# Reordering the first DMA issues of a fused attention and soft mixture-of-experts kernel

## The chip, the cores and the metric

The kernel runs on one core of a Trainium2 chip. The metric is the device time of one execution in microseconds (us); the times given are medians over a few executions. TensorE (PE) multiplies matrices, with its weight loads shown apart as PEld; VectorE (DVE), ScalarE (ACT) and GpSimd (POOL) do the element work; SyncE (SP) only issues DMAs here, and ScalarE's queue can issue DMAs as well. In the profile, SP's DMA queue is q1 and ScalarE's is q10.

## The reference

```python
# q, k, v: (4, 5056, 256) float32; tau: a scalar (1.0)
qn = q / (np.linalg.norm(q, axis=1, keepdims=True) + 1e-06)
kn = k / (np.linalg.norm(k, axis=1, keepdims=True) + 1e-06)
s = kn.transpose(0, 2, 1) @ qn / tau            # (4, 256, 256)
a = softmax(s, axis=-1)
x = (v @ a).reshape(4 * 5056, 256)
# phi: (256, 32); w1: (8, 256, 1024); w2: (8, 1024, 256)
logits = x @ phi
d = softmax(logits, axis=0)
slot_input = (d.T @ x).reshape(8, 4, 256)
slot_out[e] = np.maximum(slot_input[e] @ w1[e], 0) @ w2[e]   # e = 0..7
out = softmax(logits, axis=1) @ slot_out.reshape(32, 256)
```

The softmaxes subtract the maximum and add 1e-9 to the sum. Everything is in float32.

## The kernel before

The rows of q and k are cut into 40 **units** (ten for each of four batches). A unit is one tile `raw` of 128 partitions, four row groups `j` of q and k side by side: 8 KB a partition, 1 MB in all. Five buffers of `raw` exist (`NRAW = 5`), so units 0 to 4 are loaded at once and each later load waits until its buffer's readers are done. For each unit:

- ScalarE squares the whole tile into `sq` (line 203) for the column norms, and VectorE adds the squares up (line 209).
- Of units 1 to 39, row groups 0 and 1 are split into a rounded part (ScalarE, `cast`, line 182) and a rest (VectorE, `low`, line 188), both in the tile `hl`; three products on `hl` replace one on `raw`.
- TensorE adds the products of k and q into the score bank `S` (line 226), directly from `raw` for the row groups that are not split. Unit 0 has none split (`NS[0] = 0`): its eight products, in order of `j`, all read `raw`. A float32 product stands in the trace as two records of a weight load and two of a matmul.

In between run the loads of v and of its transpose (lines 128 and 134), the softmax over the scores, the logits, the gather of the slots, and at the end the two layers of the experts (`w1`, line 626; `w2`, line 631), the output products (line 712), their copies to SBUF on ScalarE and VectorE (lines 734 and 736) and the stores (lines 742 and 744).

The work of the main part is entered in a list `plan` by `at(key, function, arguments)`, and issued in the order of the written-out list `ORDER` of indices into `plan`. What stands outside the plan is issued ahead of it: the loads of units 0 to 4 first, then a few constants and `act.activation(warm, ...)`, which loads ScalarE's function table (line 154). Each engine, and each DMA queue, takes its own instructions in the order in which they are issued.

Three places matter here. Unit 0 is loaded in two parts, row group 0 by ScalarE's queue and groups 1 to 3 by SP's (line 141). A burst of `WAKE = 6` products of a tile of ones (`wake`, line 749) is entered first in the plan; nothing reads its result. The small tile `few_sb` holds phi, a selection mask and tau for each partition, 268 bytes a partition; it is loaded on SP by `load_few` (line 139), entry 646 of the plan, which stands 52nd in `ORDER`. Its first reader is VectorE's reciprocal of tau (line 258), and then TensorE's product with phi (line 319).

Of the kernel before, what the change touches and what calls it, by code (L numbers as in the profile page):

```python
# [8 lines left out]
F32 = mybir.dt.float32  # L9
# [7 lines left out]
P, S, G = 128, 32, 4  # L17
UB = 10
PB = 5
UT = 512  # L20
WAKE = 6
PITCH = 128
NU = B * UB
NRAW = 5
# [4 lines left out]


ORDER = [
# [46 lines left out]
]  # L78


# [1 line left out]
def colnorm_attention_soft_moe(  # L82
# [15 lines left out]
    pe, act, dve, pool, sp = nc.tensor, nc.scalar, nc.vector, nc.gpsimd, nc.sync  # L98
    ctx.enter_context(tc.manual_schedule())

    const = ctx.enter_context(tc.tile_pool(name="const", bufs=1))
# [13 lines left out]
    def load_qk(u, parts=((0, 4, sp),)):  # L115
        b, i = divmod(u, UB)
        raw = apool.tile([P, 4, 2, C], F32, tag="raw", name=f"raw{u}", bufs=NRAW)
        for lo, hi, queue in parts:
            src = qk[b, i][:, : 8 * C].rearrange("p (j x c) -> p j x c", x=2, c=C)
            queue.dma_start(raw[:, lo:hi], src[:, lo:hi])  # L120
        raws[u] = raw
# [13 lines left out]
        else:  # L135
            sp.dma_start(t[:, : 8 * P - HD], vt7[b, m])

    def load_few():
        sp.dma_start(few_sb, few)

    load_qk(0, ((0, 1, act), (1, 4, sp)))
    for u in range(1, NRAW):
        load_qk(u)

# [7 lines left out]
    dve.memset(half, 0.5)  # L152
    warm = const.tile([P, 1], F32, name="warm")
    act.activation(warm, ones[:, 0:1], AF.Exp)
    few_sb = const.tile([P, 2 * S + 3], F32, name="few_sb")
    phi_sb = few_sb[:, : 2 * S].rearrange("p (n s) -> p n s", n=2)
    sel_sb = few_sb[:, 2 * S : 2 * S + 2]
    rtau = const.tile([P, 1], F32, name="rtau")
# [595 lines left out]
    def at(key, f, *a):  # L754
        plan.append((key, len(plan), f, a))

    at(-2, wake, WAKE)
    FV = 13
# [96 lines left out]
    for p in range(17):  # L855
        k = (4, 6, 8, 10, 12, 15)[p] if p < 6 else 2 * p + 7
        for h in range(2):
# [3 lines left out]
            if h:  # L861
                for m in range(2):
                    if (p, m) in LT:
                        at(k + h + 0.996 + 0.001 * m, load_vt, p, m)
    at(3.5, load_few)

    T0_ = [NU + 1.0]

# [191 lines left out]
```

## Time and profile before

| | |
|---|---|
| median of 3 runs | 288.36 us (287.0 to 289.2) |
| the profiled execution | 287.02 us |
| its span, first to last instruction | 285.2 us |
| TensorE / VectorE / ScalarE busy | 249.9 / 236.5 / 185.0 us |
| moved by DMA | 115.61 MB, 405 GB/s on average |
| mean granted TensorE clock | 0.961 |

A profile page belongs to one execution. Times inside it count from the first instruction, and the 1.8 us between the span and the execution's time lie around it. In the page's slices, each digit is the busy share of one fortieth of the span in tenths. In a timeline row the first number is the start, the second the duration from the first to the last of the merged instructions, then engine, line, operation, tiles and count; the bracket tells how long the engine was idle before and what ended that. ACTq and SPq are the sequencers of ScalarE and SyncE, where DMAs are issued. In rows of groups, after the bar, stand the busy time and the mean duration of one in ns.

### The profile page before, as it was taken

To read this page: it belongs to the slowest core of one execution; us is meant where nothing else is said; L and a number is where in the kernel's file an instruction comes from. 1 tells how busy PE (TensorE), PEld (TensorE's weight loads), DVE (VectorE), ACT (ScalarE), POOL (GpSimd) and SP (SyncE) were. 2 spreads that over 40 slices of the span, in tenths; PEclk is the share of its full clock that TensorE was granted. 3 is DMA by queue.
4 is the path that set the end of the run, shared out by engine and by line. 5 is a ranking of instruction groups with operands and counts; after the bars stand their busy time and mean duration, and the time that the engine had idled before them with its cause. 6 is when DMAs were issued, how large, how long until landed. Compare 5 with 4: busy or idle time off the path is not lost. (4 is left out here: it accounts for less than half of the span.)

```text
span 285.2 us, 6082 instructions
## 1 busy us (share of the span) xinstructions
PE 249.9 (88%) x2446; PEld 202.5 (71%) x2446; DVE 236.5 (83%) x389; ACT 185.0 (65%) x264; POOL 9.8 (3%) x10
## 2 busy tenths in 40 slices
PE   5999999999999999999999999999889898984000
PEld 5899999897898978878778686786454777753000
DVE  1699999899999999999999999978768688994100
ACT  3978897889899796687777967175613436862200
POOL 0000002200003000000200000100000000000000
PEclk9999999999999999999999999999999999999555
DMA  7999999999999999999999999999999998999995
GB/s 277 426 411 421 413 425 420 420 417 418 400 418 388 419 434 419 416 408 410 418 398 418 411 418 430 421 425 418 422 412 415 413 371 325 407 423 416 424 424 244
DMA packets 20044, 115.61 MB, mean 405 GB/s; under 512 B 2352, under 2 KB 2352, under 8 KB 9520
## 3 DMA queue, kind: packets, MB, share of 16 engines
q1 hardware_dynamic: 19872, 114.96, 98.1%
q8 instruction: 19, 0.31, 0.4%
q10 hardware_dynamic: 144, 0.26, 0.3%
q14 instruction: 9, 0.07, 0.1%
HBM read 94.24 MB, written 20.97 MB: 404 GB/s over the span
## 5 line engine op out<-in xcount | busy, mean ns | idle before, releaser
L209 DVE TENSOR_TENSOR sq<-sq,sq 128x1024 f32<-128x1024 f32 (+1 forms) x63 | 85.3, 1367 | 1.3 <-ACT sq L203 0.6
L203 ACT ACTIVATE sq<-raw 128x2048 f32<-128x2048 f32 x40 | 76.3, 1911 | 14.5 <-DVE sq L209 5.8
L226 PE MATMUL S<-raw 128*128 128x256 f32 x328 | 81.6, 391 | 1.9 <-DMA raw<-in_qk_dram 1.9
L226 PE MATMUL S<-hl 128*128 128x256 f32 x468 | 71.0, 297 | 0.1
L226 PEld LDWEIGHTS S<-raw 128*128 128x128 f32 x328 | 60.5, 195 | 12.3 <-issue 3.3
L226 PEld LDWEIGHTS S<-hl 128*128 128x128 f32 x468 | 61.1, 190 | 3.2 <-issue 1.2
L188 DVE TENSOR_TENSOR hl<-raw,hl 128x1024 fp32r<-128x1024 f32 x39 | 47.0, 1215 | 7.1 <-ACT hl L182 7.1
L182 ACT CAST hl<-raw 128x1024 fp32r<-128x1024 f32 x39 | 40.2, 1042 | 3.3 <-PE S L226 2.6
L736 DVE COPY o<-op_None 128x512 f32<-128x512 f32 x30 | 18.7, 676 | 7.9 <-issue 7.2
L734 ACT COPY o<-op_None 128x512 f32<-128x512 f32 x30 | 15.8, 593 | 12.5 <-issue 8.2
L712 PE MATMUL op_None<-so,cT 32*128 32x256 f32 x240 | 18.6, 401 | 1.9 <-ACT o L734 1.3
L485 PE MATMUL G<-v,dn 128*32 128x256 f32 x320 | 20.1, 382 | 0.1
L712 PEld LDWEIGHTS op_None<-so,cT 32*128 32x128 f32 x240 | 14.6, 184 | 5.6 <-ACT o L734 2.7
L378 PE MATMUL L<-vt,M 128*32 128x256 f32 (+1 forms) x272 | 17.7, 380 | 0.9 <-ACT M L332 0.9
L356 ACT COPY vt<-vTp 128x512 f32<-128x512 f32 x18 | 10.4, 584 | 11.3 <-PE vTp L351 11.3
L248 POOL TENSOR_TENSOR rn<-rn,half 128x4 f32<-128x4 f32 x4 | 9.1, 2264 | 173.7 <-DVE rn L243 173.7
L485 PEld LDWEIGHTS G<-v,dn 128*32 128x32 f32 x320 | 10.0, 109 | 6.6 <-issue 0.5
L351 PE MATMUL vTp<-ident,v 128*128 128x128 f32 x96 | 14.2, 277 | 0.1
L378 PEld LDWEIGHTS L<-vt,M 128*32 128x32 f32 x272 | 8.1, 109 | 6.9 <-ACT M L332 1.3
L351 PEld LDWEIGHTS vTp<-ident,v 128*128 128x128 f32 x96 | 11.0, 142 | 2.6 <-issue 1.2
L399 ACT COPY lt<-L 128x256 f32<-128x256 f32 x20 | 7.2, 372 | 7.6 <-DVE mxs L405 3.4
L734 ACT COPY o<-op 128x256 f32<-128x256 f32 x20 | 6.3, 380 | 7.1 <-PE op L712 7.1
(111 smaller groups left out, 249.3 us busy)
## 6 DMA issues: line engine op xcount, KB each, us to landing
raw<-in_qk_dram SPq DMA_DIRECT2D x39, 1024.0 KB, 8.4
v<-in_v_dram SPq DMA_DIRECT2D x20, 1024.0 KB, 9.8
out_dram<-o SPq DMA_DIRECT2D x15, 1024.0 KB, 12.3
vt<-in_vt_dram SPq DMA_DIRECT2D x21, 512.0 KB, 8.4
w<-in_moe_w_dram SPq DMA_DIRECT2D x8, 1024.0 KB, 13.9
w<-in_moe_w_dram SPq DMA_DIRECT2D x16, 512.0 KB, 10.0
out_dram<-o SPq DMA_DIRECT2D x10, 512.0 KB, 4.2
vt<-in_vt_dram SPq DMA_DIRECT2D x4, 480.0 KB, 8.8
```

The source lines that it names most:

```text
L182: act.copy(hl[:, :ns, 0::2, :], raws[u][:, :ns])
L188: dve.tensor_tensor(hl[:, :ns, 1::2, :], raws[u][:, :ns], hl[:, :ns, 0::2, :].bitcast(F32), op=ALU.subtract)
L203: act.activation(sq, raws[u], AF.Square)
L209: dve.tensor_tensor(a[:, lo:hi], a[:, lo:hi], s[:, lo:hi], op=ALU.add)
L226: pe.matmul(sm, w, x, start=first, stop=False, skip_group_check=True)
L351: pe.transpose(tp[:, P * jj : P * jj + P], vs[p][:, 4 * h + jj, P * m : P * m + P], ident)
L356: act.copy(x[:, h * UT : h * UT + UT], tps[p, h, m])
L378: pe.matmul(L[S * g : S * g + S, :n, :], M[:, m, :], x[:, :n, S * g : S * g + S], start=m == 0, stop=m == 1,)
L485: pe.matmul(gp[S * g : S * g + S, :C], dn[:, x, j, :], vt[:, j, :], start=x == 0 and j < G, stop=x == n - 1 and j >= G,)
L712: pe.matmul(ops[b, p, hf, g][:, h, :], cT[b][S * g : S * g + S, 4 * i : 4 * i + 4, :].rearrange("s j t -> s (j t)"), so[S * g : S * g + S] ...
L734: act.copy(dst, src)
L736: dve.tensor_copy(dst, src)
```

## The change

The load of `few_sb` moves out of the plan to the very front, onto ScalarE's queue, as its first DMA. Unit 0 is cut in the middle: SP's queue opens with row groups 0 and 1, and ScalarE issues groups 2 and 3 behind `few_sb`. The plan's entry for `load_few` is gone, so the indices above 646 in `ORDER` fall by one; the order of all the other entries is the same as before. `WAKE` goes from 6 to 5.

```diff
-WAKE = 6
+WAKE = 5
...
 ORDER = [
-    ... 49, 44, 646, 52, 58, ...
+    ... 49, 44, 52, 58, ...
...
-    def load_few():
-        sp.dma_start(few_sb, few)
-
-    load_qk(0, ((0, 1, act), (1, 4, sp)))
+    few_sb = const.tile([P, 2 * S + 3], F32, name="few_sb")
+    act.dma_start(few_sb, few)
+    load_qk(0, ((0, 2, sp), (2, 4, act)))
     for u in range(1, NRAW):
         load_qk(u)
...
     act.activation(warm, ones[:, 0:1], AF.Exp)
-    few_sb = const.tile([P, 2 * S + 3], F32, name="few_sb")
     phi_sb = few_sb[:, : 2 * S].rearrange("p (n s) -> p n s", n=2)
...
-    at(3.5, load_few)
```

90 rows, old and new, of the table ORDER are left out of this document.

## The prediction

> **What bounds the kernel now.** I read the page first: the span and its busy lines, then its slices.
>
> ```profile
> span 285.2 us, 6082 instructions
> PE 249.9 (88%) x2446; PEld 202.5 (71%) x2446; DVE 236.5 (83%) x389; ACT 185.0 (65%) x264; POOL 9.8 (3%) x10
> PE   5999999999999999999999999999889898984000
> DVE  1699999899999999999999999978768688994100
> DMA  7999999999999999999999999999999998999995
> ```
>
> Three resources are full side by side: TensorE and VectorE from the second slice to about the thirtieth, the DMA engines from the second to the last. A table of stretches separates the stages (columns: PE, PEld, DVE, ACT, POOL busy, TensorE clock, DMA share, GB/s).
>
> ```profile
> 1.70:2.80 1.10, 1.10 (x7) 1.10 (x7) 0.59 (x6) 0.95 (x2) 0.00 (x0) 1.00 0.84 143
> 2.80:5.80 3.00, 1.18 (x6) 0.88 (x5) 0.00 (x0) 0.00 (x0) 0.00 (x0) 1.00 1.04 428
> 16.00:72.00 56.00, 55.88 (x382) 50.60 (x381) 54.27 (x51) 47.47 (x45) 3.07 (x1) 1.00 1.01 419
> 92.00:228.00 136.00, 132.10 (x1358) 100.29 (x1357) 124.77 (x236) 86.48 (x143) 2.99 (x2) 1.00 1.02 417
> 228.00:248.00 20.00, 18.20 (x375) 15.07 (x370) 17.25 (x40) 12.18 (x32) 0.00 (x0) 1.00 0.92 363
> 248.00:280.00 32.00, 10.67 (x138) 8.18 (x130) 13.10 (x24) 9.67 (x19) 0.00 (x0) 0.73 1.01 422
> ```
>
> From 16 to 72 us TensorE idles 0.12 us of 56 and VectorE 1.73 us, with DMA at 419 GB/s. From 248 us on the stores drain at 422 GB/s and nothing but the queue matters. Only between 228 and 248 us does DMA fall, to 363 GB/s, because stores wait for output tiles. So the end is the moment at which the output tiles are made, plus a fixed drain, and that moment is the end of a chain that runs through TensorE from its first product. A gain at the head reaches the end only if TensorE, VectorE and the load stream all let it through.
>
> The change touches the head alone. Its timeline:
>
> ```profile
> 0.73 0.40 ACTq L120 DMA_DIRECT2D raw<-in_qk_dram  x1
> 0.74 13.95 SPq L120 DMA_DIRECT2D raw<-in_qk_dram  x7
> 1.05 2.93 PE L749 MATMUL wake<-ones 128*128 128x128 f32 x12 [1.05 <-DVE half L152]
> 1.17 1.28 ACT L154 ACT_TABLE_LOAD   x1 [1.17 <-PEq L1017]
> 2.46 0.20 ACT L154 ACTIVATE warm<-ones 128x1 f32<-128x1 f32 x1
> 5.85 1.91 ACT L203 ACTIVATE sq<-raw 128x2048 f32<-128x2048 f32 x1 [3.19 <-DMA raw<-in_qk_dram]
> 5.87 10.14 PE L226 MATMUL S<-raw 128*128 128x256 f32 x36 [1.89 <-DMA raw<-in_qk_dram]
> 8.14 1.04 ACT L182 CAST hl<-raw 128x1024 fp32r<-128x1024 f32 x1 [0.38 <-DMA raw<-in_qk_dram]
> 11.03 2.29 DVE L209 TENSOR_TENSOR sq<-sq,sq 128x2048 f32<-128x2048 f32 x1 [0.59 <-ACT sq L203]
> ```
>
> TensorE runs the products of ones until 3.98 us, idles 1.89 us and starts when unit 0 is there; ScalarE starts with it, then idles 0.38 us for unit 1. VectorE follows ScalarE. From here TensorE has no idle time in the timeline.
>
> **The change, part by part.**
>
> *The split of unit 0.* Both of its DMAs leave within 0.01 us of each other and land 4.9 and 5.1 us later, at about 5.64 and 5.83 us:
>
> ```profile
> L120 SPq DMA_DIRECT2D raw<-in_qk_dram x5: 371/424/779, 0.7 to 2.9; - x5
> DMA to landing us min/median/max: 4.9/5.0/5.1
> q1 hardware_dynamic: 116, 0.71, 69.5%
> q10 hardware_dynamic: 108, 0.22, 21.1%
> ```
>
> The last two rows are the DMA view from 1.6 to 4.7 us: SP's queue (q1) had moved 116 packets and ScalarE's (q10) 108, though SP's are 6 KB and ScalarE's 2 KB. The engines take one packet of each in turn, so a queue's share goes with its packet size, and three quarters and one quarter end together. The Trainium skill, "DMA: Bandwidth & Descriptors", section "Queues, rings and completion order", also has round robin, but says that an engine drains a group of 9 to 17 descriptors before it switches. By that, each engine would finish SP's rows before it looked at ScalarE's, which is rival 1; the near-equal counts above speak against it.
>
> Afterwards both halves are 0.524 MB in 4 KB packets, so they take equal turns, and unit 1 follows on SP in 8 KB packets. ScalarE's half goes out one issue later, by the 424 ns of an issue on SP. In that time SP gets ahead by 0.42 us at 143 to 428 GB/s (the first two rows of the table), 0.06 to 0.18 MB. Its half then lands that much sooner than the pair does now, 0.14 to 0.42 us. ScalarE's half has the same amount left when unit 1's packets, twice as large, begin to take turns with it: it needs three times the time for it and lands 0.28 to 0.85 us later than 5.83.
>
> *phi and tau first.* The same small load sits at 24.0 us today:
>
> ```profile
> L139 SPq DMA_DIRECT2D few_sb<-in_few_dram x1: 433/433/433, 24.0 to 24.0; - x1
> L258 DVE RECIPROCAL rtau<-few_sb x1: 131/131/131, 51.9 to 51.9; 128x1 f32<-128x1 f32 x1
> DMA packets 250, 0.77 MB, mean 386 GB/s; under 512 B 160, under 2 KB 160, under 8 KB 160
> ```
>
> The third row is the stretch 29.6 to 31.6 us, in which it passed: 386 GB/s in place of 419, and 34 KB of it its own, so (0.84 - 0.77 + 0.034) MB / 0.42 MB per us = 0.25 us of stream at most; its bytes alone are 0.08 us. At the head it may hide wholly in the slow 143 GB/s of the first microsecond: 0 to 0.25 us, I take 0.1. After 32 us this cancels, since it no longer stands in SP's queue; only the landings before that are later by it. On SP 433 ns of issue go away at 24.0 us; SP waits on buffers there, so I give it nothing (0.43 us at most, if SP were late). First use is at 51.9 us, so no reader is hurt. On ScalarE one more issue, about 0.4 us, moves the table load from 1.17 to about 1.6 us; the 3.19 us of idle before 5.85 us hide it, and without that cover it would cost its 0.4 us.
>
> *Sum at the head.* TensorE's first products need SP's half alone: start 5.87 - (0.14 to 0.42) + (0 to 0.25), that is 5.45 to 5.98; I take 5.67, 0.2 us earlier, near the middle. The products on ScalarE's half come 8 loads later, 3.2 us at the 0.4 us of a load worked out below, near 8.9, and don't wait. ScalarE's square needs both halves: 6.1 to 6.9 us, I take 6.4. It then ends 0.55 us later, of which 0.38 us of idle swallow most: the cast, and VectorE behind it, are 0.17 us later (0 to 0.7 at the ends). VectorE has 1.73 us of idle before 72 us for that.
>
> *One product of ones less.* A product is two of the twelve records, about 0.45 us of 2.93; the burst ends near 3.5 us and nothing waits for it. What it could change is the rate that follows. The same shape before and after about 10 us (xcount, busy, mean ns):
>
> ```profile
> L226 PEld LDWEIGHTS S<-raw 128*128 128x128 f32 x10 | 3.2, 332 | 2.9 <-DMA raw<-in_qk_dram 2.2
> L226 PEld LDWEIGHTS S<-raw 128*128 128x128 f32 x25 | 4.8, 190 | 0.7
> ```
>
> Ten loads start in the 3.9 us from 5.87 to 9.8, 0.4 us apiece; 25 in the 5.3 us from 10.3 to 15.6, 0.21 apiece. So TensorE starts unit 0 at half rate despite six products and gets its full rate some 4 us later: about 10 x 0.2 = 2 us are lost there, whatever the burst did. I take 0 for the product; bounds are 0 and +2 us (rival 3). The Trainium skill, "TensorE: Matmul & The Clock Gate", Part 1, says that the clock opens only after a free-running window of about 3.4 us of sustained work. By it neither 2.93 nor 2.5 us of ones opens it; the slow start of this trace agrees.
>
> The 0.2 us at TensorE is worth 0.1 if the rate changes at the same moment (half rate until then), 0.2 if the change moves with the start. What is late next is the load stream, which is no earlier than before:
>
> ```profile
> 231.19 2.83 PE L673 MATMUL O<-w,hT 128*32 128x128 f32 x96
> L631 SPq DMA_DIRECT2D w<-in_moe_w_dram x1: 328/328/328, 221.3 to 221.3; - x1
> DMA to landing us min/median/max: 10.0/10.0/10.0
> ```
>
> The last second-layer weights land at 231.3 us, inside the run of products that uses them: a few tenths of gain fit, more would wait here. **Sum: -0.1 us** (-0.4 to +0.4). The profiled execution took 287.02 us; the median of the three runs is 288.36 (287.0 to 289.2), and since the sum is a difference I set it against the median: **288.2 us**.
>
> **The rivals.**
>
> 1. *SP's half first, whole.* If engines serve several rows of a queue per turn, SP's half lands 0.524 MB / 428 GB/s = 1.2 us sooner and TensorE starts at 4.65. For it: SP's queue has the earlier packets. Against: the 116 to 108 packets. Worth 0.6 (rate change fixed) to 1.2 us, if the last weights let it through: 287.5, 287.2 at best.
> 2. *ScalarE's half last (the slower side).* Nothing keeps it from being squeezed by unit 1 until that lands at 8.14 us. It decides from a landing after 6.2 us, when the 0.38 us of idle are gone; from there each tenth delays ScalarE and VectorE by a tenth, up to 8.14 - 5.85 - 0.38 = 1.9 us. For it: VectorE is 97% busy from 16 to 72 us. Against: 1.73 us idle there. At half of 1.9 us: 289.4; at most 290.3.
> 3. *The missing product counted.* If six products open the full rate in some executions and five never do, those lose up to 2 us: 289 to 290.4. For it: the runs are 2.2 us apart, about as much. Against: this execution stayed slow after six.
> 4. *It does nothing:* both halves land together near 5.9 us, as now, because few's small packets and the second issue shift both: 288.4.
>
> **How the numbers follow.** Forecast 0.50, rival 1 0.14, rival 2 0.14, rival 3 0.05, rival 4 0.17. A measurement here can tell about 1%, 2.9 us, from no change, and the runs themselves scatter by 2.2 us, so a median of few runs adds about 0.7 to each side of -0.4 to +0.4: 287.3 to 289.5. Rival 4 lies within that; rival 1 with half that scatter takes the range to 286.8, and rival 2's middle to 289.7. Faster than 285.5 needs rival 1 and with it an earlier change of rate (1.2 + 2 us): 0.03. Slower than 291.2 needs rivals 2 and 3 together: 0.04. Within 1%: 0.93.
>
> **What would show it.** Right: TensorE's first product on unit 0 between 5.4 and 5.9 us with the wake burst ending near 3.5; ScalarE's first square at 6.1 to 6.9; the cast of unit 1 at 8.2 to 8.4; slow loads until about 10 us; phi's line gone from SP. Wrong: a start before 5 us (rival 1); a square after 7 us, with VectorE's first sum past 12 us (rival 2); another count of slow loads (rival 3). The prediction fails if the stretch from 228 to 248 us has more idle DMA than now, since a tenth at the head would then not be what sets the end.

## The result: slower by 1.0%, outside the range

The changed kernel took 290.56 us as the median of 7 runs, the kernel before 287.46 us beside it. The ratio is 1.0103 (95% interval 1.0068 to 1.0138), that is 3.0 us more (2.0 to 4.0). Forecast were 288.2 us and 286.8 to 289.7; as a difference, -0.1 us. Ratios, here and below, leave out executions that took over 1.5% more than the fastest of their kernel; medians do not.

The profiled execution of the changed kernel took 294.24 us. TensorE's granted clock was 0.50 in it from 205.5 to 212.3 us and from 219.2 to 222.6 us, and the profile of before has no such stretch behind its head. So the head of the changed kernel is read from this profile, and the end from a second one (291.11 us), which has one such stretch, from 215.2 to 218.6 us.

The head, as a timeline of the changed kernel (start, duration, engine, line, operation):

```profile
0.73 0.41 ACTq L137 DMA_DIRECT2D few_sb<-in_few_dram  x1
1.05 2.50 PE L745 MATMUL wake<-ones 128*128 128x128 f32 x10 [1.05 <-DVE half L149]
1.17 0.45 ACTq L118 DMA_DIRECT2D raw<-in_qk_dram  x1
1.65 1.28 ACT L151 ACT_TABLE_LOAD   x1 [1.65 <-PEq L1012]
4.86 2.08 PE L222 MATMUL S<-raw 128*128 128x256 f32 x4 [1.31 <-DMA raw<-in_qk_dram]
8.83 5.49 PE L222 MATMUL S<-raw 128*128 128x256 f32 x12 [1.89 <-DMA raw<-in_qk_dram]
8.87 1.91 ACT L199 ACTIVATE sq<-raw 128x2048 f32<-128x2048 f32 x1 [5.72 <-DMA raw<-in_qk_dram]
10.69 1.03 ACT L178 CAST hl<-raw 128x1024 fp32r<-128x1024 f32 x1
13.56 2.29 DVE L205 TENSOR_TENSOR sq<-sq,sq 128x2048 f32<-128x2048 f32 x1 [0.59 <-ACT sq L199]
```

TensorE starts earlier than before, at 4.86 us against 5.87, but does only four of unit 0's sixteen records and stops until 8.83. ScalarE's square starts at 8.87 instead of 5.85, the cast at 10.69 instead of 8.14, VectorE's first sum at 13.56 instead of 11.03. Everything that needs the second half of unit 0 is 2.5 to 3.0 us late. The loads of `raw` issued in the first 1.5 us say why: SP's half and SP's unit 1 in the first row, ScalarE's half in the second.

```profile
L118 SPq DMA_DIRECT2D raw<-in_qk_dram x2: 382/402/422, 0.7 to 1.2; - x2
L118 ACTq DMA_DIRECT2D raw<-in_qk_dram x1: 453/453/453, 1.2 to 1.2; - x1
DMA to landing us min/median/max: 4.1/7.4/7.6
```

4.1 us after its issue at 0.74 SP's half is there (4.82 in the trace); unit 1 takes 7.4 and lands at 8.62; ScalarE's half, issued at 1.17, takes 7.6 and lands at 8.79, behind a unit twice its size. The bytes that each queue (q1 SP, q10 ScalarE) had moved from 1 to 4.2 us, before and then changed:

```profile
q1 hardware_dynamic: 93, 0.57, 56.9%
q10 hardware_dynamic: 81, 0.17, 16.0%
```

```profile
q1 hardware_dynamic: 159, 0.67, 68.6%
q10 hardware_dynamic: 137, 0.03, 4.9%
```

Before, both queues moved a part of unit 0 side by side. Changed, SP's queue had moved nearly all of its half (0.524 MB) and begun with unit 1, while ScalarE's had moved 137 packets with 0.03 MB. That is phi's size (128 rows of 268 bytes): nothing of the half yet. From 4.2 us on the half then shares the engines with unit 1. The DMA view from 5 to 7 us:

```profile
q1 hardware_dynamic: 66, 0.54, 63.7%
q10 hardware_dynamic: 72, 0.29, 35.8%
```

The counts are near equal, 66 to 72, with 8 KB packets on one side and 4 KB on the other.

The delay then stays. The score products on `hl` that start after about 150 us (shortest, median and longest duration in ns, first and last start in us), before, and in the second profile of the changed kernel:

```profile
L226 PE MATMUL S<-hl x84: 278/283/469, 151.6 to 188.3; 128*128 128x256 f32 x84
```

```profile
L222 PE MATMUL S<-hl x89: 278/283/469, 149.7 to 190.9; 128*128 128x256 f32 x89
```

The last of them starts 2.6 us later. Between the head and there, nothing is made up and nothing more is lost. Stretches of that second profile, with the columns of the stretches shown of before:

```profile
16.00:72.00 56.00, 55.89 (x364) 51.08 (x366) 54.48 (x51) 48.18 (x45) 3.06 (x1) 1.00 1.01 409
228.00:248.00 20.00, 17.43 (x417) 14.52 (x412) 15.84 (x38) 9.28 (x28) 0.00 (x0) 1.00 0.83 328
248.00:280.00 32.00, 14.96 (x192) 11.53 (x184) 17.38 (x31) 13.42 (x26) 0.00 (x0) 0.79 1.01 421
```

From 16 to 72 us TensorE idles 0.11 us of 56 and VectorE 1.52, much as before (0.12 and 1.73). From 228 to 248 us the DMA engines move 328 GB/s instead of 363, and TensorE has 4.3 us more left for the drain (14.96 to 10.67). More idle DMA in that stretch is what the prediction named as its own failure. These two profiled executions lie 4.1 us apart: 2.6 are there at 191 us, and the rest comes behind it, where the second profile has its 3.4 us at half the clock.

### The profile page after: what moved, and what is told of

It reads as the page before. It is cut to its first block, busy times and chain, and to the rows that moved or that the text cites. A ratio compares the mean times of both kernels' runs of the same rounds, so it can differ in the third digit from the quotient of the medians.

```text
span 292.5 us, 6079 instructions
## 1 busy us (share of the span) xinstructions
PE 256.1 (88%) x2444; PEld 204.4 (70%) x2444; DVE 236.7 (81%) x389; ACT 185.0 (63%) x264; POOL 9.7 (3%) x10
## 5 line engine op out<-in xcount | busy, mean ns | idle before, releaser
L222 PE MATMUL S<-raw 128*128 128x256 f32 x328 | 83.5, 397 | 3.2 <-DMA raw<-in_qk_dram 3.2
L222 PEld LDWEIGHTS S<-raw 128*128 128x128 f32 x328 | 61.3, 198 | 14.6 <-DMA raw<-in_qk_dram 4.2
L481 PE MATMUL G<-v,dn 128*32 128x256 f32 x320 | 22.0, 409 | 0.0
L481 PEld LDWEIGHTS G<-v,dn 128*32 128x32 f32 x320 | 10.6, 117 | 7.8 <-issue 2.1
```

The source lines that it names most:

```text
L222: pe.matmul(sm, w, x, start=first, stop=False, skip_group_check=True)
L481: pe.matmul(gp[S * g : S * g + S, :C], dn[:, x, j, :], vt[:, j, :], start=x == 0 and j < G, stop=x == n - 1 and j >= G,)
```

## The experiments

Two questions were open: which part of the change makes ScalarE's half late, and why 2.5 us at the head arrive whole at the end. The theories have letters in the expectations: **T**, phi's many small packets take turns that the half needs; **O**, the half has lost its place in the order of issue, and SP's next load has taken it; **Q**, what counts is to be a queue's first DMA; **V**, ScalarE and VectorE carry the delay to the end; **P**, TensorE does. "First sum" below is the start of VectorE's first sum of squares (11.03 us before), "17th record" the start of TensorE's 17th matmul record on unit data (11.53 us before), and "lands" the landing of ScalarE's part of unit 0 (5.83 us before). Ratios are to the kernel before in the same call (medians 287.3 to 287.9 us).

### Which part of the change

**The changed kernel once more**, unedited, for its end:

> The changed kernel once more, for a second profile: ScalarE's half of unit 0 near 8.8 us, the first square right behind it, VectorE's first sum near 13.5 us, 290.5 us.

291.11 us; first sum 13.75, 17th record 14.05, lands 8.97. The head is the same as in the first profile, to 0.2 us.

**Phi behind the half** instead of ahead of it, the rest as changed:

```diff
-    act.dma_start(few_sb, few)
     load_qk(0, ((0, 2, sp), (2, 4, act)))
+    act.dma_start(few_sb, few)
```

> The changed kernel with ScalarE's two issues swapped: its half of unit 0 first, phi and tau behind it. Theory T (turns): the engines take one packet of each queue in turn, whatever its size, so phi's eight small packets an engine, standing first, cost ScalarE's queue the eight turns in which SP's half goes through; with phi behind, both halves share from the start and land between 5.5 and 5.9 us, ScalarE's first square starts there and the time is that of the kernel before, 287.5 us (286.8 to 288.2). Theory W (the missing product of ones delays TensorE's full rate): the time stays near 290.5 us, since WAKE is still 5.

287.76 us, ratio 0.9998 (0.9969 to 1.0027). Its timeline, and its queues from 1 to 4.2 us:

```profile
0.73 0.40 ACTq L118 DMA_DIRECT2D raw<-in_qk_dram  x1
1.16 0.45 ACTq L138 DMA_DIRECT2D few_sb<-in_few_dram  x1
5.76 1.91 ACT L199 ACTIVATE sq<-raw 128x2048 f32<-128x2048 f32 x1 [2.62 <-DMA raw<-in_qk_dram]
11.24 2.29 DVE L205 TENSOR_TENSOR sq<-sq,sq 128x2048 f32<-128x2048 f32 x1 [0.59 <-ACT sq L199]
```

```profile
q1 hardware_dynamic: 107, 0.44, 43.1%
q10 hardware_dynamic: 80, 0.33, 26.4%
```

Exchanging the two issues on ScalarE, 0.43 us apart, takes the whole loss away. Phi still leaves at the head, in the same bytes and packets; so neither its place at the head nor the split in halves costs anything that shows.

**The three parts alone.** The burst of ones, added back to the changed kernel and taken from the kernel before; the halves without phi's move; phi's move with the old split.

```diff
 # changed kernel
-WAKE = 5
+WAKE = 6
```

> The changed kernel with six products of ones again. T: nothing comes back, 290.5 us (290 to 291), with ScalarE's half of unit 0 landing near 8.8 us. W: all of it comes back, 287.5 us.

```diff
 # kernel before
-WAKE = 6
+WAKE = 5
```

> The kernel before with one product of ones less and nothing else. T: no difference, 287.5 us (286.8 to 288.2), with slow weight loads until about the same time as before. W: 290.5 us.

```diff
 # kernel before
-    load_qk(0, ((0, 1, act), (1, 4, sp)))
+    load_qk(0, ((0, 2, sp), (2, 4, act)))
```

> The kernel before with one edit: unit 0 cut in the middle, row groups 0 and 1 on SP, 2 and 3 on ScalarE; phi and tau stay at their old place, six products of ones. Theory T (one packet of each queue in turn): equal packets, equal turns, both halves land at 5.5 to 5.9 us and the time is 287.5 us (286.8 to 288.2). If it is the cut itself that costs (two halves of 4 KB packets, one on each queue): 290 us or more, with ScalarE's half landing after 8 us.

```diff
 # kernel before; the plan's load_few is gone
+    act.dma_start(few_sb, few)
     load_qk(0, ((0, 1, act), (1, 4, sp)))
```

> The kernel before with one edit: phi and tau are ScalarE's first DMA; the old split (row group 0 on ScalarE, 1 to 3 on SP) and six products of ones stay. T: SP's three quarters use up the eight turns of phi and land near 4.9 us; ScalarE's quarter then takes turns with unit 1's 8 KB packets and lands near 8.3 us. Since TensorE's first product reads row group 0, all of TensorE starts near 8.3 us in place of 5.87, so this is as slow as the changed kernel or slower: 290 to 291.5 us. W: 287.5 us, since all six products are there.

| | median us | ratio (95%) | first sum | 17th record | lands |
|---|---|---|---|---|---|
| changed, WAKE 6 | 290.55 | 1.0086 (1.0052 to 1.0119) | 13.72 | 14.27 | 8.94 |
| before, WAKE 5 | 287.58 | 1.0007 (0.9979 to 1.0035) | 10.96 | 11.14 | 5.63 |
| before, halves | 288.21 | 1.0014 (0.9985 to 1.0042) | 11.20 | 11.44 | 5.78 |
| before, phi first | 291.05 | 1.0106 (1.0069 to 1.0143) | 14.01 | 14.27 | 9.24 |

The sixth product of ones changes nothing in the time that shows, in either direction, nor do the halves. Phi ahead of unit 0 costs the same 1% with the old split, where ScalarE's part is a quarter in 2 KB packets: it lands at 9.24 us, SP's three quarters at 5.88.

### Why the half is late

**Half of phi**, the other half on SP behind unit 4: T expects half the loss.

```diff
 # changed kernel
-    act.dma_start(few_sb, few)
+    act.dma_start(few_sb[:64], few[:64])
...
+    sp.dma_start(few_sb[64:], few[64:])
```

> The changed kernel with only the first 64 partitions of phi and tau ahead of ScalarE's half; the other 64 follow on SP behind unit 4. T: four turns of small packets in place of eight, so when SP's half is through, half of ScalarE's half is left, and that shares with unit 1: it lands near 7.2 us (8.8 with eight turns, 5.7 with none). ScalarE's first square starts there, 0.38 us of the delay are swallowed ahead of the cast, VectorE is about 1 us late: 288.5 us (288 to 289). If the cost were that of a second issue on ScalarE, whatever its size: as the changed kernel, 290.5 us.

A miss: 291.31 us, 1.0154 (1.011 to 1.0199), first sum 14.51, 17th record 14.50, and the half lands at 9.74, later rather than sooner. The issue of half of phi took 0.55 us where that of the whole took 0.41, so the half's issue came at 1.32 us, 0.15 us behind that of unit 1, and took 0.60 us itself; its first packet came at 5.17 us. T, which counts packets, has no place for this; O expects a half that is issued behind unit 1 to be late. Why the smaller piece takes longer to issue stays open.

**The same bytes in 16 rows**, into a spare tile; the real phi stays at its old place on SP:

```diff
 # kernel before, with the halves
+    spare = const.tile([16, 8 * (2 * S + 3)], F32, name="spare")
+    act.dma_start(spare, few.rearrange("(a b) c -> a (b c)", a=16))
     load_qk(0, ((0, 2, sp), (2, 4, act)))
```

> The kernel before with the middle cut of unit 0, six products of ones, phi and tau at their old place, and ScalarE's first DMA a spare copy of the same 34 KB in 16 rows of 2144 bytes, one packet an engine, which nothing reads. Theory T (a packet is a turn): one turn in place of eight, so ScalarE's half lands near 6.0 us and the time is that of the kernel before, 287.5 us (286.8 to 288.3). Theory I (any small DMA ahead on ScalarE's queue holds the half back, by its issue or its landing): ScalarE's half lands near 8.8 us or later and the time is 290 us or more.

290.93 us, 1.0123 (1.0073 to 1.0174): as slow, though the first DMA now has 16 long rows in place of 128 short ones. Its timeline, and its queues from 1 to 4.2 us:

```profile
0.73 0.41 ACTq L142 DMA_DIRECT2D spare<-in_few_dram  x1
1.18 0.44 ACTq L120 DMA_DIRECT2D raw<-in_qk_dram  x1
8.66 1.91 ACT L205 ACTIVATE sq<-raw 128x2048 f32<-128x2048 f32 x1 [5.52 <-DMA raw<-in_qk_dram]
```

```profile
q1 hardware_dynamic: 167, 0.71, 71.8%
q10 hardware_dynamic: 32, 0.03, 4.6%
```

32 packets with the 0.03 MB of the spare tile, which were through by about 3.0 us, and none of the half before 4.2. T as the cause falls. What is left is that the half is ScalarE's *second* DMA (Q), or that it is issued no sooner than SP's unit 1 (O).

**The half as ScalarE's first DMA, but issued behind unit 1.** It waits for a small write of VectorE to its own tile:

```diff
 # kernel before
-    load_qk(0, ((0, 1, act), (1, 4, sp)))
+    load_qk(0, ((0, 2, sp),))
...  # units 1 to 4 on SP, then the constants
+    dve.memset(raws[0][:, 2, 0, :], 0.0)
+    act.dma_start(raws[0][:, 2:4], ...)   # row groups 2 and 3 of unit 0
```

> The kernel before with the middle cut of unit 0 and phi at its old place; ScalarE's half is its first DMA, but waits for a small VectorE write, so that it is issued near 1.4 us, between SP's second (unit 1, 1.16) and third. O: it starts after 4 us, behind the preparation of unit 1, and lands after 8 us; 290 us or more. Q: as a first DMA it starts about 1.3 us after its issue, near 2.7 us, and lands near 6.1 us; 287.6 us (287 to 288.4).

291.82 us, 1.0137 (1.0085 to 1.019). Its timeline, and its queues from 1 to 4.2 us:

```profile
0.73 2.47 SPq L120 DMA_DIRECT2D raw<-in_qk_dram  x5
1.32 0.37 ACTq L154 DMA_DIRECT2D raw<-in_qk_dram  x1
10.06 1.91 ACT L205 ACTIVATE sq<-raw 128x2048 f32<-128x2048 f32 x1 [6.83 <-DMA raw<-in_qk_dram]
```

```profile
q1 hardware_dynamic: 166, 0.70, 68.6%
```

No phi is ahead of it and its queue was empty; its issue at 1.32 us, 0.15 us after unit 1's, is enough: there is no row for ScalarE's queue at all, its first packet came at 4.58 us and it landed at 9.97. To be first on its queue does not help the half, so Q falls as the cause.

**SP held back.** From the other side: the changed kernel, phi's 128 packets still ahead of the half, but SP issues units 1 to 4 only from 2.21 us on, since the first of them waits for a small write of VectorE.

```diff
 # changed kernel: unit 1 is gated
     def load_qk(u, parts=((0, 4, sp),), gate=False):
+        if gate:
+            dve.memset(raw[:, 0, 0, 0:1], 0.0)
...  # the loop now stands behind the constants
     for u in range(1, NRAW):
-        load_qk(u)
+        load_qk(u, gate=u == 1)
```

> The changed kernel (phi's 128 small packets ahead of ScalarE's half, five products of ones), in which SP issues units 1 to 4 only after a small VectorE write near 2.2 us. If O is the only cause, ScalarE's half lands near 6 us and the time is 287.5 us. If phi's eight turns also count by themselves (theory T), the half starts only when they are through, near 4 us, takes turns with unit 1 and lands after 8 us: 290 us.

288.42 us, 1.0025 (0.9992 to 1.0058). Its timeline, and its queues from 1 to 4.2 us:

```profile
1.17 0.45 ACTq L120 DMA_DIRECT2D raw<-in_qk_dram  x1
2.21 1.77 SPq L120 DMA_DIRECT2D raw<-in_qk_dram  x4
6.08 1.91 ACT L201 ACTIVATE sq<-raw 128x2048 f32<-128x2048 f32 x1 [2.94 <-DMA raw<-in_qk_dram]
11.82 2.29 DVE L207 TENSOR_TENSOR sq<-sq,sq 128x2048 f32<-128x2048 f32 x1 [0.59 <-ACT sq L201]
```

```profile
q1 hardware_dynamic: 143, 0.52, 50.3%
q10 hardware_dynamic: 179, 0.19, 17.2%
```

SP's queue stops at its 0.52 MB, ScalarE's gets 0.16 MB of the half through by 4.2 us, and it lands at 5.99 instead of 8.79. Phi's packets are all still there. The first sum is 0.8 us later than before, since unit 1 itself lands late now (8.85 us against 8.12), and the time, 0.7 us more (-0.2 to 1.7), says no more than that.

**The same gate on the kernel with the spare tile**, the real phi at its old place:

```diff
 # the kernel of 16 rows, with the gate; the loop behind the constants
-        load_qk(u)
+        load_qk(u, gate=u == 1)
```

> The run with the spare copy of 16 rows ahead of ScalarE's half, in which SP issues units 1 to 4 only after a small VectorE write near 2.2 us, so that ScalarE's second DMA (1.17 us) goes out ahead of SP's second. Theory O (order of issue: the half starts late because the load of unit 1, issued on SP a hair earlier, is prepared first): ScalarE's half now starts by 3 us and lands near 5.9 us; 287.5 us (286.9 to 288.3). Theory Q (a second DMA on ScalarE's queue starts some 3 us after its issue, whatever SP does): it still starts near 4.1 us and lands after 7 us; 289.5 us or more.

The landing came at 6.57 us instead of 8.58, with the half's first packet at 3.57 us: nearer to O (by 3 us, 5.9) than to Q (near 4.1, after 7), but later than O has it. The time did not come back: 290.59 us, 1.0082 (1.0049 to 1.0116), which is Q's figure, though not on Q's path. Unit 1 landed only at 9.61 here, so the cast that waits for it began at 9.69 and the first sum at 12.57, 1.5 us late. The gate had moved the wait by one unit, and units 1 to 4 all landed 1.4 to 1.5 us later than before. The 2.4 us (1.4 to 3.3) are more than that 1.5, and what the rest is stays open.

ScalarE's part of unit 0 in these runs, in us from the start of the span:

| | on ScalarE's queue | its issue starts | unit 1's issue starts | its first packet | lands |
|---|---|---|---|---|---|
| before (a quarter) | first | 0.73 | 1.16 | 1.99 | 5.83 |
| phi behind | first | 0.73 | 1.16 | 2.14 | 5.73 |
| changed | second | 1.17 | 1.17 | 4.32 | 8.79 |
| 16 rows | second | 1.18 | 1.16 | 4.21 | 8.58 |
| half of phi | second | 1.32 | 1.17 | 5.17 | 9.74 |
| first, but behind unit 1 | first | 1.32 | 1.17 | 4.58 | 9.97 |
| changed, SP held back | second | 1.17 | 2.21 | 3.66 | 5.99 |
| 16 rows, SP held back | second | 1.17 | 2.21 | 3.57 | 6.57 |

So the cause is settled as far as the order of issue goes: the half must be issued clearly before SP's next load. Level with it is not enough. In both profiles of the changed kernel the half's issue even starts a little ahead, by 0.005 and 0.009 us, and ends 0.03 us after unit 1's; the half was late all the same. Not shown is what stands between an issue and its first packet. SP's first DMA had packets 1.0 us after its issue, ScalarE's first in these kernels after 1.3 to 2.1 us (2.4 with half of phi), the half as ScalarE's second not before 2.4 us even with SP's unit 1 held back. The preparation of a DMA leaves no record in the trace.

### Why it reaches the end

**ScalarE and VectorE late alone.** The square of unit 0 is done twice, into the same tile:

```diff
 # kernel before
+        if u == 0:
+            act.activation(sq, raws[u], AF.Square)
         act.activation(sq, raws[u], AF.Square)
```

> The kernel before, in which ScalarE squares unit 0 twice into the same tile (the second overwrites the first with the same values). Unit 0 lands and TensorE starts as before; ScalarE is 1.91 us later less 0.38 us of idle, and VectorE with it, 1.5 us. Theory V (the end hangs on the chain of ScalarE and VectorE, which starts with the first square): all of it arrives, 289.0 us (288.7 to 289.4). Theory P (the end hangs on TensorE's start on row groups 2 and 3): 287.5 us.

288.38 us, 1.0051 (1.0026 to 1.0076), that is 1.5 us (0.7 to 2.2): the difference that V gives, though the time is under V's 288.7 to 289.4. Its timeline, and its last score products:

```profile
7.74 1.91 ACT L205 ACTIVATE sq<-raw 128x2048 f32<-128x2048 f32 x1
12.43 2.29 DVE L211 TENSOR_TENSOR sq<-sq,sq 128x2048 f32<-128x2048 f32 x1 [0.59 <-ACT sq L203]
```

```profile
L228 PE MATMUL S<-hl x84: 274/283/467, 152.6 to 189.6; 128*128 128x256 f32 x84
```

TensorE keeps its start (17th record at 11.52). The second square takes 1.91 us; the 0.38 us of idle before the cast take some of it, and the first sum is 1.4 us late. The last score product is 1.3 us late, and the time 1.5. VectorE's idle time absorbed next to nothing of it.

**TensorE late alone.** 32 products of ones in place of 6:

```diff
 # kernel before
-WAKE = 6
+WAKE = 32
```

> The kernel before with 32 products of ones in place of six: they keep TensorE until 9.5 to 11.5 us, so its 17th record on unit 0 and 1 starts at 13 to 15 us, as in the changed kernel (14.1) and not as before (11.5), while ScalarE squares unit 0 at 5.85 us as before. P: as slow as the changed kernel, 289.5 to 290.5 us. V: no more than 0.5 us are lost, 287.5 to 288 us, since TensorE catches up with VectorE within the first units.

289.34 us, 1.0073 (1.0044 to 1.0102), 2.1 us (1.3 to 2.9). V's small figure was missed, P's about right. Its timeline, and its last score products:

```profile
1.05 9.83 PE L749 MATMUL wake<-ones 128*128 128x128 f32 x64 [1.05 <-DVE half L152]
10.72 4.48 PE L226 MATMUL S<-raw 128*128 128x256 f32 x20
11.10 2.29 DVE L209 TENSOR_TENSOR sq<-sq,sq 128x2048 f32<-128x2048 f32 x1 [0.59 <-ACT sq L203]
```

```profile
L226 PE MATMUL S<-hl x90: 274/283/469, 149.7 to 190.8; 128*128 128x256 f32 x90
```

VectorE is on time, TensorE's 17th record 2.6 us late (14.17), the last score product 2.5. TensorE holds the buffers of `raw`: SP issues unit 5 at 14.4 us here, at 11.8 before. Either chain, late by itself, is late at the end; in the changed kernel both are.

The granted clock differs from execution to execution, and this shows in the times. Of the 89 executions of the kernel before in the four calls, the 56 with a mean clock of 0.959 or more have a median of 286.9 us, the 33 others 288.6. With 0.959 or more alone, phi first on the old split has 289.7 us (5 executions), the square done twice 288.25 (8) and 32 products of ones 289.35 (6). These are 2.8, 1.3 and 2.4 us more than before, for 3.0, 1.4 and 2.6 us at the head.

**Both early.** Units 0 and 1 come in two halves each, all on SP, and the first square is done in two halves; then the same with 8 products of ones:

```diff
 # kernel before; the second one with WAKE = 8
-    load_qk(0, ((0, 1, act), (1, 4, sp)))
-    for u in range(1, NRAW):
+    for u in range(2):
+        load_qk(u, ((0, 2, sp), (2, 4, sp)))
+    for u in range(2, NRAW):
...
+        if u == 0:
+            for h in (0, 2):
+                act.activation(sq[:, h : h + 2], raws[u][:, h : h + 2], AF.Square)
```

> A version meant to start all three engines earlier: units 0 and 1 in two halves each, all on SP in order; the first square in two halves; phi at its old place; six products of ones. The first half of unit 0 should land near 4.5 us, the second near 5.7, the first half of unit 1 near 6.9; TensorE starts 1.2 us earlier, the cast of unit 1 starts near 7.0 in place of 8.14, VectorE's first sum near 10.1 in place of 11.0. If the head sets the end, as the other runs say, 286.5 us (286.0 to 287.0); if the load stream holds the gain back, 287.3 us.

> The same with eight products of ones, so that TensorE is busy without a gap from 1.05 us until the first half of unit 0 is there, and gets its full rate by 8 us at the latest and not near 10. TensorE's 17th record starts near 8.5 to 10 us (11.5 before). If TensorE's rate at the head matters beside ScalarE and VectorE, 0.3 to 0.6 us less than with six products; if VectorE alone sets the pace, the same as with six.

287.68 us, 1.0003 (0.9969 to 1.0038), and 287.63, 0.9997 (0.9967 to 1.0028): no gain shows, though the intervals leave room for 0.9 us. First sums at 10.84 and 10.17, 17th records at 8.91 and 9.24, so both chains are 0.2 to 2.6 us earlier there. The second one's timeline, and its last score products:

```profile
4.63 5.64 PE L231 MATMUL S<-raw 128*128 128x256 f32 x20
10.17 2.29 DVE L214 TENSOR_TENSOR sq<-sq,sq 128x2048 f32<-128x2048 f32 x1 [0.91 <-ACT sq L208]
10.74 1.99 PE L231 MATMUL S<-raw 128*128 128x256 f32 x8 [0.47 <-DMA raw<-in_qk_dram]
```

```profile
L231 PE MATMUL S<-hl x84: 277/283/472, 150.8 to 187.6; 128*128 128x256 f32 x84
```

TensorE's lead meets the load stream at once: unit 2 lands at 10.69 us, no sooner than before (10.62), and TensorE waits for it, and again for unit 3. 0.7 us of the gain are there at 188 us. The last second-layer weights are issued that much sooner (220.60 us against 221.32), but land at 231.39, against 231.36 before: the load stream ends no sooner. That it holds the gain back fits this trace, but is not shown. The clock of this execution was 0.50 from 211.8 to 215.2 us, and 8 of the 12 executions of either kernel had a mean clock below 0.959, against the 33 of 89 before. The four others of each have medians of 286.3 and 286.65 us, 0.6 and 0.3 us under the 286.9 of before, so a part of the gain may have passed and been lost to the clock. Delays passed; a gain did not show in either median, and no version was clearly faster than the kernel before.

## Why the prediction was wrong

- **Phi ahead of the half: the step that failed.** It was priced as bytes ("0 to 0.25 us, I take 0.1") and as an issue by which "SP gets ahead by 0.42 us at 143 to 428 GB/s", 0.06 to 0.18 MB. SP was 0.67 MB ahead at 4.2 us, and the half landed at 8.79, where 6.1 to 6.9 was the range. The rate of one packet in turn was applied from the moment of issue, as if the half's packets stood ready then; in fact unit 1, issued on SP at 1.17 us, level with the half, had its first packets at 3.7 us, and the half at 4.32. Phi behind the half, and SP held back, both bring the landing back (5.73 and 5.99).
- **Rival 2 named the right mechanism and the right side, with too low a chance (0.14) and bound.** "Until that lands at 8.14 us" took unit 1's landing of before; unit 1 lands at 8.62 when the half shares the engines with it, and the half later still. So the square was 3.0 us late, the cast 2.55 and the time 3.0, where 1.9 and 290.3 were the most. "From there each tenth delays ScalarE and VectorE by a tenth" held.
- **"VectorE has 1.73 us of idle before 72 us for that" was wrong.** VectorE late by 1.4 us cost 1.5 (the square done twice). What VectorE waited for from 16 to 72 us, before (in all, times, longest, in us):

```profile
DVE rn L252 <- POOL rn L248: 0.9, 1, 0.9
DVE hl L188 <- ACT hl L182: 0.2, 1, 0.2
```

  The first is a wait for GpSimd, which itself waits for VectorE (line 243), the second one for ScalarE, which was late as well; the rest are short gaps. Such waits move along with the delay: in the kernel that squares twice, VectorE still idles 1.50 us of that stretch. Whoever counts an engine's idle time as slack must ask what it waits for.
- **TensorE's start** came at 4.86 us, before the 5.45 to 5.98 of the forecast and near rival 1's 4.65, though for another reason: not several rows a turn, but no packets beside SP's half except phi's small ones. "The products on ScalarE's half come 8 loads later" was wrong twice: that half came too late for any order, and the products don't run in the order of the row groups, though the description of the kernel says so. `ORDER` begins `1, 0, 2, 5, 3, 4`, and entries 2 to 5 are unit 0's row groups 0 to 3: group 3, of ScalarE's half, stands second, behind four records. TensorE waited 1.89 us for it and lost the early start again.
- **One packet of each queue in turn** was right: 66 to 72. The Trainium skill, "DMA: Bandwidth & Descriptors", section "Queues, rings and completion order", has 9 to 17 descriptors drained from a ring before the switch; these counts of 4 and 8 KB rows don't agree.
- **The product of ones at nothing** was right for the time, in both kernels (0.9979 to 1.0035 alone; 1.0086 with six and 1.0103 with five in the changed one). That TensorE starts unit 0 at half rate "whatever the burst did" was not right. The weight loads of the changed kernel from 4.8 to 14 us (all 16 on unit 0 and one more), and its first four with six products, from 4.8 to 5.7 us (count, busy, mean ns):

```profile
L222 PEld LDWEIGHTS S<-raw 128*128 128x128 f32 x17 | 5.4, 331 | 5.4 <-DMA raw<-in_qk_dram 4.2
L222 PEld LDWEIGHTS S<-raw 128*128 128x128 f32 x4 | 0.7, 189 | 1.3 <-DMA raw<-in_qk_dram 1.2
```

  With six, the first four ran at the full rate, as rival 3 has it, so 2.93 us of ones were enough there; then TensorE waited 3 us for the half, and nearly all loads from 8.98 us on took 337 ns again. The slow loads last until 14.4 us with five products and until 14.7 with six, so rival 3 is not the cause of the loss.

- **The load stream as what holds a gain back** was not tested here, since nothing was gained; the two early kernels are in line with it, and don't prove it. It was used as a bound for gains only; that the end follows a late head in full was said in the first part ("a chain that runs through TensorE from its first product") and then not applied to a late half.

## What to carry to other kernels

When a DMA is put ahead of another on a queue, ask which loads of the *other* queues are issued before the displaced one then, and give it their whole length, not only its neighbour's bytes. The DMA that the first work waits for is issued first on its queue and ahead of any large load elsewhere; a small load that is needed late goes behind it. Where several full engines feed each other, price a delay and a gain apart: here a delay of either engine arrived at the end almost whole, and an earlier head brought no gain that showed.

## What was not expected of the hardware

- 0.43 us in the order of issue moved a landing by 3.1 us (5.73 to 8.79). The Trainium skill, "DMA: Bandwidth & Descriptors", section "Issuing engines are not separate DMA queues", says that issuing from several engines saves only the sequencer's time. The traces agree that the queues share their engines (66 to 72 packets side by side); but who issued first decided 1% of the time here.
- The time from the start of an issue to its first packet was 1.0 us for SP's first DMA and 1.3 to 2.4 us for ScalarE's, both issued at 0.73 us, and 2.4 to 3.9 us for a half issued by ScalarE at 1.17 to 1.32 us: 2.4 and 2.5 with SP held back, 3.0 and more level with SP's unit 1 or behind it.
- Where TensorE started before 5 us, its loads on unit 0 were down at 190 ns by the fourth in four of five kernels with six products of ones, and in none of the four profiles with five. In the changed kernel this made no difference to the time.
- 64 records of ones took 9.83 us, 154 ns apiece, 12 of them 2.93 us, 244 apiece: in the long burst TensorE reached its full rate on its own, and the 21 loads after it took some 190 ns apiece. It was of no use, since the burst itself was in the way.
